# Order of GpSimd's work at the gate's maximum, and where the next pass's x operands are made, in an attention + MLP + mixture-of-experts kernel

## The chip, the cores and the metric

One Trainium2 chip, one of its cores. The time of a kernel is in microseconds of the device (us), the median of several executions. One further execution was taken with the hardware profiler, and every row below comes from that one.

## The reference

Three stages follow one another (2304 tokens, 512 features). The change lies in the third.

```python
x = block_causal_attention(q, k, v)          # 4 x 8 heads x 576 x 64 -> 2304 x 512
h = x @ w_in;  x = np.maximum(0.01 * h, h) @ w_out
# experts, E = 8, F = 1024
logits = x @ w_gate
logits = logits - logits.max()               # one maximum over all tokens and experts
P = np.exp(logits)
for _ in range(8):
    P /= P.sum(1, keepdims=True) + 1e-09
    P /= P.sum(0, keepdims=True) + 1e-09
    P *= N / E
for e in range(E):
    out += P[:, e:e+1] * (np.maximum(x @ w1[e], 0.0) @ w2[e])
```

## The kernel before, in words

All products are made from split operands: a value is kept as a high part (rounded by ScalarE) and a low part (the rest, by VectorE), and three matmuls stand for one. In the rows `xh…`, `w1h`, `w2h` are high parts and `xl…`, `w1l`, `w2l` low parts.

**Experts.** The tokens are cut into `NPASS` = 3 passes of 768. A group is an expert and a quarter of its F (256 columns); a pass has 32 groups, worked through in 16 rounds of two (`n` and `n + 1`, the loop at the end). A round has two halves. The *first products* (`first`, `product`, L851) make x @ w1 by a scheme with seven products in place of eight, so 14 products of 6 matmuls a round. Their x operands are called A11, S1, S2, S3, S4, A12 and A22 (`terms`); `x_step(p, k)` makes one of them for pass p: ScalarE's high part, VectorE's low part, and with `make` a VectorE subtraction of x blocks before it (`x_src`). `quarter` (first pass) takes the results "22", "12", "21" and "11" from PSUM: VectorE adds a kept part (L868, tile `c`), ScalarE makes the high part of the ReLU (L874), VectorE the low part (L875). The *second products* multiply by w2: in the first pass `combine` (L1075), six tiles of 12 matmuls a round into four PSUM banks; in the later passes `seventh` (L1019), seven products again, except in the last round of each pass (`closing`), which uses `combine`.

**Weights in the first pass.** w1 and w2 of each group are loaded raw, split, turned into the sums that the seven-product scheme wants, and also written to DRAM for the passes behind. For w2: `w2_load` fetches 512 KB into the one buffer that the group's parity has, `w2_split` makes high and low parts (L129, L130), `w2_more` makes four sums of quarters in place on GpSimd (L740 to L743), `w2_away` splits those sums (L782 ScalarE, L783 VectorE, two of each) and stores them with `keep_parts` (L703). Only then can `w2_load` of the group two further on reuse the buffer. All loads and stores are issued on SyncE's queue.

**The gate.** In the first round of pass one (`n == 0`) the last logits are made between the first products. `gate_max` (after product 3) reduces on VectorE (`gmax`, L653) and across partitions on GpSimd (`gall`, L654). `normal` then runs the exponential and the first row sums (L657 to L668), and the 8 normalisations follow between later matmuls.

**Order.** The program is written in one order, and a scheduler with a timing model of its own settles each engine's order, so an instruction can stand on its engine ahead of one that was written before it. TensorE's order is pinned by `in_order`. `tc.issue_after(t)` keeps what is written under it behind instruction t on t's engine; `behind(...)` does that with the last quarter's two instructions (`last_taken`), and `next_on` pins the order of the later passes. Each engine runs its queue in order.

Of the kernel before, what the change touches and what calls it, by code (L numbers as in the profile page):

```python
# [15 lines left out]
P = 128  # L16
# [20 lines left out]
def block_attention_mlp_moe(  # L37
# [15 lines left out]
    nc = tc.nc  # L53
# [50 lines left out]
    def w_load(which, e, j, pool=None):  # L104
        raw = (pool or rawpool).tile([P, 1024], F32, name="wraw", tag="wraw")
        f0 = 2 * j * P
        if which == 1:
            src = w1[e - 1][:, f0:f0 + 2 * P]
            nc.sync.dma_start(
                out=raw.rearrange("p (c f) -> p c f", c=KC), in_=src.rearrange("(c p) f -> p c f", p=P)  # L110
            )
        else:
            nc.sync.dma_start(
                out=raw.rearrange("p (j d) -> p j d", j=2),
                in_=w2[e - 1][f0:f0 + 2 * P, :].rearrange("(j p) d -> p j d", p=P),
            )
        w_raw[which, e, j] = raw
# [359 lines left out]
    turned = const.tile([P, 32], F32, name="ramp_t")  # L477
# [55 lines left out]
    for w in (1, 2):  # L533
# [22 lines left out]
    st = {  # L556
        n: const.tile([P, w], F32, name=n)
        for n, w in (("gmax", 1), ("gall", 1), ("gneg", 1), ("rs", TT), ("cs", E), ("cr", E))
    }
# [91 lines left out]

    def gate_max():
        nc.vector.tensor_reduce(out=st["gmax"], in_=pr, axis=AX.XY, op=ALU.max)  # L653
        nc.gpsimd.partition_all_reduce(st["gall"], st["gmax"], P, bass.bass_isa.ReduceOp.max)  # L654

    def gate_exp():
        nc.vector.tensor_scalar(out=st["gneg"], in0=st["gall"], scalar1=-1.0, scalar2=None, op0=ALU.mult)  # L657
# [35 lines left out]
    terms = ("A11", "S1", "S2", "S3", "S4", "A12", "A22")  # L693
# [20 lines left out]
    def w2_load(n):  # L714
        if n < N0:
            w_load(2, 1 + groups[n][1], groups[n][2], raw2[n % 2])
# [3 lines left out]
    def w2_split(n):  # L720
        if n < N0:
            key = (2, 1 + groups[n][1], groups[n][2])
            w2_raw[n] = w_raw[key]
            w_split(*key)
            parts = w_part[key]
            keep_parts(2, n, 0, [x[:, DM:DM + HD] for x in parts], HD, DM, DM + HD)
            keep_parts(2, n, 1, [x[:, 0:DM] for x in parts], DM, DM, 2 * DM)
            if groups[n][1:] in ((E - 1, NI - 2), (E - 1, NI - 1)):
                keep_parts(2, n, 2, parts, 2 * DM)
# [5 lines left out]
    def w2_more(n):  # L735
        if n >= N0:
            return
        raw = w2_raw[n]
        b21, b22, b11, b12 = (raw[:, c * HD:(c + 1) * HD] for c in range(4))
        nc.gpsimd.tensor_tensor(out=b11, in0=b12, in1=b11, op=ALU.subtract)  # L740
        nc.gpsimd.tensor_tensor(out=b12, in0=b22, in1=b12, op=ALU.subtract)
        nc.gpsimd.tensor_tensor(out=b22, in0=b22, in1=b11, op=ALU.subtract)
        nc.gpsimd.tensor_tensor(out=b21, in0=b22, in1=b21, op=ALU.subtract)  # L743

    def w2_away(n):
        if n >= N0:
            return
        raw = w2_raw.pop(n)
        for part, x in ((0, raw[:, DM:2 * DM]), (1, raw[:, 0:DM])):
            pool, tag = ((mpool, "th"), (rawpool, "wb"))[part]  # L750
            hi = pool.tile([P, DM], F32R, name=tag, tag=tag, bufs=1)
            lo = x.bitcast(F32R)
            halves(hi, lo, x)
            keep_parts(2, n, part, (hi, lo), DM, 0)
# [78 lines left out]
    def x_step(p, k, make=True):  # L833
        src = x_src(p, k, make)
        hi, lo = (xpart.tile([P, 2, HT], F32R, name=f"x{n}{k}", tag=f"x{n}{k}") for n in "hl")
        put = next_on if tails else lambda f, **k: f(**k)
        put(nc.scalar.copy, out=hi, in_=src)
        put(nc.vector.tensor_tensor, out=lo, in0=src, in1=f32(hi), op=ALU.subtract)
        bq[p, k] = (hi, lo)
# [43 lines left out]
    def behind(*steps):  # L883
        with ExitStack() as order:
            for t in last_taken:
                order.enter_context(tc.issue_after(t))
            for s in steps:
                s()
# [331 lines left out]
    turned = False  # L1220
    done = 0
    for n in range(0, NGR, 2):
        p, e, i = groups[n]
        turn = closing(n) and p + 1 < NPASS
        for m in range(done, len(first_products)):
            first(n, m)
            if n == 0 and 0 < m <= TC // 2:
                in_order(gate_chunk)(NPASS - 1, TC // 2 + m - 1, o_bank())
            if p == 0:
                if n == 0 and m == 2:  # L1230
                    w2_split(n + 1)
                if n == 0 and m == 4:
                    w2_more(n + 1)
                if m in ((1, 3) if n else (2, 8)):
                    w2_away(n + m // 3 % 2 if n else n + m // 8)
                    w2_load(n + 2 + (m // 3 % 2 if n else m // 8))
                if m == 5:
                    w1_sums(n + 2)
            if turned and 2 < m < 6:
                x_step(p, terms[m + 1])  # L1240
            if n == 0 and m == TC // 2:
                gate_max()
            if norm and m in ((2, 6) if n else (5,)):
                normal(o_bank)
            if not norm and not owed and rows_owed and m == 8:
                in_order(gate_rows)(o_bank, rows_owed.pop(0))
            if turn and p == 0 and m == 2:
                x_step(p + 1, "A11")
                for k in ("S1", "S3"):
                    x_src(p + 1, k, True)  # L1250
            if m == 5:
                for g in range(2):
                    w1_fetch(n + 2 + g, 0)
            if p and closing(n) and 7 <= m < 7 + TC:
                turn_back(order[m - 7])
        if done and m == 13:
            for g in range(2):
                w1_fetch(n + 2 + g, 0)
        for g in range(2):
            w1_fetch(n + 2 + g, 1)  # L1260
        if owed and not norm:
            behind(settle)
        if n == 4:
            nc.sync.dma_start(out=x_away, in_=xa[2])
        done = 0
        if p and not closing(n):
            for k in ("A11", "S2"):
                for g in range(2):
                    (parted if k == "A11" else summed)(n + g, k)
            for j in range(len(sevens)):  # L1270
                for c in range(2):
                    seventh(n, j, c)
                    beside_seventh(n, j, c)
                if j < 6:
                    first(n + 2, j)
                if closing(n + 2):
                    join(j)
                if j == 0 and groups[n + 2][1] != e:
                    row_load(p, e + 1)
                if j == 2:  # L1280
                    for g in range(2):
                        w2_fetch(n + 2 + g, 0)
            for g in range(2):
                w2_fetch(n + 2 + g, 1)
            if closing(n + 2) and p + 1 < NPASS:
                nc.sync.dma_start(out=xa[2], in_=x_away)
            done = 6
            turned = False
            continue
        more = [  # L1290
            lambda: (w1_s(n + 2), w1_a(n + 2)),
            lambda: (w1_sums(n + 3), w1_load(n + 4)),
            lambda: (w1_s(n + 3), w1_a(n + 3)),
            lambda: (w1_load(n + 5), w2_split(n + 2)),
            lambda: (w2_more(n + 2), w2_split(n + 3)),
            lambda: w2_more(n + 3),
        ]
        for m, t in enumerate(order):
            combine(n, t)
            if norm and m in (1, 4):  # L1300
                normal(h_bank)
            if p == 0:
                behind(more[m])
            if turn and p == 0 and m < 3:
                behind(lambda: x_step(p + 1, terms[m + 1], m == 1))
            if turn and p and m < 4:
                x_step(p + 1, terms[m], m == 2)
                if m == 0:
                    for k in ("S1", "S3"):
                        x_src(p + 1, k, True)  # L1310
        if turn:
            if p == 0:
                for pool in (raw2[1], mpool, raw2[0]):
                    pool.release()
                tpool = tc.alloc_tile_pool(name="tpool", bufs=1, reuse_waits="tile")
                lay_out()
            for part in range(2):
                for g in range(2):
                    w2_fetch(n + 2 + g, part)
            row_load(p + 1, 0)  # L1320
        turned = turn
# [33 lines left out]
```

## Time and profile before

| | |
|---|---|
| Time, median of 3 executions | 2084.09 us (2083.12 to 2084.18) |
| Time of the profiled execution | 2082.56 us |
| Its span, first to last instruction | 2080.7 us |
| TensorE busy | 2056.3 us, 99% of the span |
| VectorE, ScalarE, GpSimd busy | 1567.5, 836.7, 660.7 us |
| Mean granted TensorE clock | 0.996 of full speed |
| DMA | 436.88 MB, mean 210 GB/s |

The experts begin about 603 us into the span; the first pass ends at about 1127 us, the second at about 1602 us. Busy time says which engine worked; the waits say what it stood still for, and in order of time they say what stood ahead of what on an engine.

### The profile page before, as it was taken

The page shows a single profiled execution, that of the slowest core. Times are in us where ns is not written, and L with a number is a line of the kernel's source. Part 1 is how long each engine was busy: PE and PEld are TensorE (multiplying, and loading weights), DVE is VectorE, ACT ScalarE, POOL GpSimd, SP SyncE. Part 2 cuts the span into 40 slices and gives each one's busy share as a digit, 9 for nine tenths or more (in the row PEclk, how much of TensorE's full clock was granted, in tenths as well). Part 3 has the DMA queues.
Part 4 walks back from the last instruction along what each step waited for, and adds up shares of the span by engine and source line. Part 5 has one row for each costly group of instructions (what it writes and reads, how often), then busy time and mean ns, then how long its engine had stood idle before and what let it go on. Part 6 is the DMA issues. An engine that isn't in the chain of part 4 may idle for free.

```text
span 2080.7 us, 31734 instructions
## 1 busy us (share of the span) xinstructions
PE 2056.3 (99%) x11196; PEld 1883.0 (90%) x11196; DVE 1567.5 (75%) x2707; ACT 836.7 (40%) x1826; POOL 660.7 (32%) x642
## 2 busy tenths in 40 slices
PE   9999999999998999999999999999999999999999
PEld 6666898988887889889898999999999999999998
DVE  7877656565467887877876688888887788888886
ACT  7776332222344454454453432323333433233322
POOL 2322212131023545534541333323331333233321
PEclk9999999999998999999999999999999999999999
DMA  5553111010056888888988677777777677777772
GB/s 139 128 125 78 41 41 51 31 51 31 1 192 223 298 294 314 304 292 309 322 300 334 244 269 251 263 255 252 272 264 277 234 251 265 254 250 274 262 258 104
DMA packets 235742, 436.88 MB, mean 210 GB/s; under 512 B 77864, under 2 KB 114728, under 8 KB 235328
## 3 DMA queue, kind: packets, MB, share of 16 engines
q1 hardware_dynamic: 234384, 434.56, 60.3%
q8 instruction: 89, 1.46, 0.3%
q14 instruction: 69, 0.57, 0.1%
q10 hardware_dynamic: 1200, 0.30, 0.1%
HBM read 308.82 MB, written 125.95 MB: 209 GB/s over the span
## 4 chain that ended last, share of the span: by engine, by line
PE 92%; DVE 4%; issue 1%; DMA 1%; POOL 1%; ACT 1%; SPq 0%; DVEq 0%; POOLq 0%; ACTq 0%
PE h_ps L851 27%; PE o L1019 21%; PE o L1075 13%; PE o L519 9%; PE h_ps L499 9%; PE sc L317 4%; PE o L851 3%; PE tr L357 2%; PE av L382 2%; DVE xa L948 1%; PE qm L291 0%; DVE w1l L783 0%; DMA k_0h<-th 0%; PE km L297 0%; PE av L379 0%
## 5 line engine op out<-in xcount | busy, mean ns | idle before, releaser
L948 DVE TENSOR_TENSOR xa<-o,xa 128x384 f32<-128x384 f32 x392 | 215.9, 552 | 110.4 <-PE o L1019 106.3
L851 PE MATMUL h_ps<-xhS,w1h 128*128 128x384 f32 x768 | 257.9, 336 | 0.0
L851 PE MATMUL h_ps<-xhS,w1l 128*128 128x384 f32 x768 | 257.0, 335 | 0.0
L851 PE MATMUL h_ps<-xlS,w1h 128*128 128x384 f32 x768 | 256.9, 335 | 0.0
L948 POOL TENSOR_TENSOR xa<-xa 128x384 f32<-128x384 f32 x92 | 106.0, 1152 | 414.0 <-DVE xa L948 373.8
L948 ACT COPY places<-h_ps 128x384 f32<-128x384 f32 x192 | 92.3, 481 | 291.5 <-PE h_ps L851 223.8
L948 ACT CAST xllate<-xa 128x384 fp32r<-128x384 f32 x120 | 61.6, 514 | 280.4 <-POOL xa L948 280.4
L851 PE MATMUL h_ps<-xhA,w1h 128*128 128x384 f32 x448 | 152.4, 340 | 14.1 <-DVE c L868 12.9
L851 PE MATMUL h_ps<-xhA,w1l 128*128 128x384 f32 x448 | 150.9, 337 | 0.0
L851 PE MATMUL h_ps<-xlA,w1h 128*128 128x384 f32 x448 | 150.9, 337 | 0.0
L851 PEld LDWEIGHTS h_ps<-xlS,w1h 128*128 128x128 f32 x768 | 144.5, 188 | 0.0
L851 PEld LDWEIGHTS h_ps<-xhS,w1h 128*128 128x128 f32 x768 | 144.5, 188 | 0.0
L851 PEld LDWEIGHTS h_ps<-xhS,w1l 128*128 128x128 f32 x768 | 144.4, 188 | 0.0
L1075 PE MATMUL o<-w2h,xhlate 128*128 128x512 f32 x408 | 143.8, 391 | 0.0
L948 POOL TENSOR_TENSOR places<-places 128x384 f32<-128x384 f32 x60 | 61.0, 1017 | 251.3 <-DVE wa L948 234.6
L1075 PE MATMUL o<-w2h,xllate 128*128 128x512 f32 x384 | 133.9, 389 | 0.0
L765 POOL TENSOR_TENSOR wa<-wraw 128x256 f32<-128x256 f32 x32 | 30.6, 957 | 306.9 <-DVE w1l L783 277.5
L1019 PE MATMUL o<-xllate,w2h 128*128 128x384 f32 x480 | 124.1, 337 | 3.0 <-DVE xllate L948 2.9
L507 DVE TENSOR_TENSOR g<-h_ps,g 128x512 f32<-128x512 f32 (+1 forms) x80 | 50.9, 636 | 96.9 <-ACT g L506 96.6
L1019 PE MATMUL o<-xhlate,w2h 128*128 128x384 f32 x480 | 121.7, 334 | 0.0
L519 PE MATMUL o<-hh,w2h 128*128 128x512 f32 (+1 forms) x320 | 117.8, 368 | 0.0
L519 PE MATMUL o<-hh,w2l 128*128 128x512 f32 (+1 forms) x320 | 117.7, 368 | 0.0
(260 smaller groups left out, 5754.4 us busy)
## 6 DMA issues: line engine op xcount, KB each, us to landing
wraw<-in_moe_w_dram SPq DMA_DIRECT2D x64, 512.0 KB, 4.5
w1h<-k_1h SPq DMA_DIRECT2D x64, 512.0 KB, 5.3
w1l<-k_1l SPq DMA_DIRECT2D x64, 512.0 KB, 6.3
w2h<-k_1h SPq DMA_DIRECT2D x60, 512.0 KB, 6.0
w2l<-k_1l SPq DMA_DIRECT2D x60, 512.0 KB, 6.9
w1h<-k_0h SPq DMA_DIRECT2D x64, 384.0 KB, 4.0
w1l<-k_0l SPq DMA_DIRECT2D x64, 384.0 KB, 4.5
w2h<-k_0h SPq DMA_DIRECT2D x60, 384.0 KB, 4.5
```

Of the source, the lines that this page charges most:

```text
L317: nc.tensor.matmul(sc, qbd[p % 2][:, i, :], kT[p % 2][:, lo:hi], start=True, stop=True)
L357: nc.tensor.transpose(tr[:, s].rearrange("p h q -> p (h q)"), ex[p % 2][:, off[i] + c * P:off[i] + (c + 1) * P], ident,)
L382: nc.tensor.matmul(av[p][r, 512 + P * max(c - 1, 0):512 + S - P], lhsT, a[:, q0:, :], start=c == 0, stop=c == NKC - 1,)
L499: nc.tensor.matmul(ps[:, 0:n], w[:, c, cols], x, start=c == 0 and s == 0, stop=c == KC - 1 and s == 2,)
L507: nc.vector.tensor_tensor(out=g[:, 0:n], in0=ps[:, 0:n], in1=g[:, 0:n], op=ALU.max)
L519: nc.tensor.matmul(ps[:, 0:n], w[:, cut], h[:, 0:n], start=start and m == 0, stop=stop and m == 2)
L765: nc.gpsimd.tensor_tensor(out=one[:, 0], in0=a21, in1=a22, op=ALU.add)
L851: mm = nc.tensor.matmul(ps, w[:, c], x[:, c], start=first and c == 0 and s == 0, stop=c == 1 and s == 2, skip_group_check=True,)
L948: ins = f(*a, **k)
L1019: mm = nc.tensor.matmul(o, a, b, start=i == 0, stop=i == 5)
L1075: mm = nc.tensor.matmul(o, h, w, start=m == 0, stop=m == 11)
```

## The change

There are two parts. **At the gate's maximum:** `gate_max` returns GpSimd's instruction, and `w2_more(1)` is written behind it with `tc.issue_after`; `w2_away(1)` and `w2_load(3)` leave the first products of round 0 (place 8) and are written behind the last quarter of that round, ahead of its second products; `w2_split(3)` is written one place later. **The x operands:** in the last round of a pass, x_step for the next pass is called at each of the six tiles of the second products, in place of three (next pass one) or four (next pass two); what is left for the first products of the next pass is A22 of the last pass, at place 1; before, S4, A12 and A22 of both passes stood there, at places 3 to 5.

```diff
     def gate_max():
         nc.vector.tensor_reduce(out=st["gmax"], in_=pr, axis=AX.XY, op=ALU.max)
-        nc.gpsimd.partition_all_reduce(st["gall"], st["gmax"], P, bass.bass_isa.ReduceOp.max)
+        t = nc.gpsimd.partition_all_reduce(st["gall"], st["gmax"], P, bass.bass_isa.ReduceOp.max)
+        return getattr(t, "ins", t)
...
-                if n == 0 and m == 4:
-                    w2_more(n + 1)
-                if m in ((1, 3) if n else (2, 8)):
-                    w2_away(n + m // 3 % 2 if n else n + m // 8)
-                    w2_load(n + 2 + (m // 3 % 2 if n else m // 8))
+                if m in ((1, 3) if n else (2,)):
+                    w2_away(n + m // 3)
+                    w2_load(n + 2 + m // 3)
                 if m == 5:
                     w1_sums(n + 2)
-            if turned and 2 < m < 6:
-                x_step(p, terms[m + 1])
+            if turned and p > 1 and m == 1:
+                x_step(p, terms[6])
             if n == 0 and m == TC // 2:
-                gate_max()
+                with tc.issue_after(gate_max()):
+                    w2_more(1)
...
-            lambda: (w2_more(n + 2), w2_split(n + 3)),
-            lambda: w2_more(n + 3),
+            lambda: (w2_more(n + 2), None if n == 0 else w2_split(n + 3)),
+            lambda: (w2_split(n + 3) if n == 0 else None, w2_more(n + 3)),
         ]
+        if n == 0:
+            behind(lambda: (w2_away(1), w2_load(3)))
         for m, t in enumerate(order):
...
-            if turn and p == 0 and m < 3:
-                behind(lambda: x_step(p + 1, terms[m + 1], m == 1))
-            if turn and p and m < 4:
-                x_step(p + 1, terms[m], m == 2)
+            if turn and p == 0:
+                behind(lambda: x_step(p + 1, terms[m + 1], m not in (0, 2)))
+            if turn and p:
+                x_step(p + 1, terms[m], m not in (1, 3))
```

## Rows read from the trace of the kernel before

**Rows 1.** The page: busy us (share of the span) xinstructions of each engine.

```profile
PE 2056.3 (99%) x11196; PEld 1883.0 (90%) x11196; DVE 1567.5 (75%) x2707; ACT 836.7 (40%) x1826; POOL 660.7 (32%) x642
```

**Rows 2.** Waits of TensorE: waiting line, releaser, total us, times, longest us.

```profile
PE h_ps L851 <- DVE c L868: 12.9, 3, 7.9
PE o L1019 <- DVE xllate L948: 2.9, 4, 1.0
PE h_ps L851 <- DVE xa L948: 1.2, 2, 0.6
```

**Rows 3.** Timeline of TensorE: start us, us, instruction, [idle before <- releaser].

```profile
619.79 0.34 PE L851 MATMUL h_ps<-xhS,w1l 128*128 128x384 f32 x1
624.74 0.69 PE L851 MATMUL h_ps<-xhA,w1h 128*128 128x384 f32 x1 [4.61 <-DVE c L868]
...
634.92 0.69 PE L851 MATMUL h_ps<-xhA,w1h 128*128 128x384 f32 x1 [7.89 <-DVE c L868]
...
641.67 0.39 PE L1075 MATMUL o<-w2h,xhlate 128*128 128x512 f32 x1
```

**Rows 4.** Chain that ended last, one later round's two halves: start us, us, what.

```profile
848.52 14.58 PE h_ps L851 x84
863.10 16.36 PE o L1075 x72
```

**Rows 5.** Timeline of GpSimd from 600 us.

```profile
601.05 0.73 POOL L768 TENSOR_TENSOR wa<-wraw,wa 128x256 f32<-128x256 f32 x1
614.96 0.74 POOL L740 TENSOR_TENSOR wraw<-wraw 128x256 f32<-128x256 f32 x1 [13.18 <-PE o L622]
622.01 0.38 POOL L654 PARTITION_ALL_REDUCE gall<-gmax  x1 [6.32 <-issue]
629.26 0.71 POOL L741 TENSOR_TENSOR wraw<-wraw 128x256 f32<-128x256 f32 x1 [6.87 <-issue]
```

**Rows 6.** Timeline of VectorE around the gate's maximum.

```profile
615.06 0.30 DVE L653 TENSOR_REDUCE gmax<-pr 128x1 f32<-128x144 f32 x1
622.42 0.15 DVE L657 TENSOR_SCALAR gneg<-gall 128x1 f32<-128x1 f32 x1 [7.06 <-POOL gall L654]
...
624.14 0.55 DVE L868 TENSOR_TENSOR c<-h_ps,s 128x384 f32<-128x384 f32 x1
...
630.82 0.69 DVE L783 TENSOR_TENSOR wraw<-wraw,th 128x512 fp32r<-128x512 f32 x1 [5.82 <-POOL wraw L742]
...
643.79 0.56 DVE L875 SCALAR_TENSOR_TENSOR xllate<-c,xllate 128x384 fp32r<-128x384 f32 x1 [0.59 <-ACT xllate L874]
```

**Rows 7.** GpSimd's sequencer, lines L654 and L331: ns min/median/max, first and last start.

```profile
L654 POOLq MODIFY_POOL_CONFIG  x2: 11/11/11, 615.6 to 615.7; - x2
L331 POOLq MODIFY_POOL_CONFIG  x2: 11/11/11, 8.8 to 8.8; - x2
```

**Rows 8.** Timeline of GpSimd at the start of the kernel.

```profile
8.08 0.54 POOL L441 COPY vraw<-nought 64x128 f32<-64x128 f32 x2
12.42 0.20 POOL L331 TENSOR_TENSOR ssum<-ssum 128x1 f32<-128x1 f32 x1 [3.80 <-ACT ex L326]
```

**Rows 9.** Stretch of one us: us, busy (x) of PE, PEld, DVE, ACT, POOL, granted clock, DMA share, GB/s.

```profile
640.00:641.00 1.00, 1.00 (x7) 1.00 (x6) 0.17 (x1) 0.28 (x1) 0.00 (x0) 0.83 0.00 0
```

**Rows 10.** Timeline of VectorE and TensorE where pass two begins.

```profile
1137.11 0.96 DVE L948 TENSOR_TENSOR xlA<-xa,xhA 128x768 fp32r<-128x768 f32 x1 [0.90 <-ACT xhA L948]
1137.98 0.55 DVE L948 TENSOR_TENSOR xa<-h_ps,places 128x384 f32<-128x384 f32 x1
...
1138.68 0.41 PE L851 MATMUL h_ps<-xhA,w1h 128*128 128x384 f32 x1 [0.58 <-DVE xa L948]
```

**Rows 11.** VectorE in a pass's last second products: us, busy (x), granted clock, DMA share, GB/s.

```profile
1590.00:1602.00 12.00, 8.69 (x11) 1.00 0.39 147
```

**Rows 12.** Timeline of ScalarE in the second products of round 0.

```profile
645.83 1.99 ACT L129 CAST w2h<-wraw 128x1024 fp32r<-128x1024 f32 x2
```

**Rows 13.** DMA issues from 570 to 720 us: what, queue, count, KB each, median us to landing.

```profile
wraw<-in_moe_w_dram SPq DMA_DIRECT2D x15, 512.0 KB, 4.3
```

## The prediction

> **What bounds the kernel now.** Read the page first: TensorE is busy for 99% of the span [rows 1]. So only what TensorE stands still for, or runs slowly through, can be won, and the next view is its waits. There are three entries of weight [rows 2]: 12.9 us for VectorE's tile `c` in the first pass, and 2.9 and 1.2 us for VectorE's results on L948. In order of time, the first is nearly all in one place: 4.61 and 7.89 us in round 0 of the experts [rows 3]. The other two are at the beginnings of passes two and three; one of the six is shown [rows 10].
>
> How large is the hole in round 0? TensorE starts the last matmul of S4 for the first group at 619.79 and the second products at 641.67 [rows 3], 21.88 us. Between lie five products of 6 matmuls (A22 twice, S4, A12 twice), so 31 steps from start to start. An undisturbed round takes 14.58 us for 84 matmuls [rows 4], 0.1736 a step, so the steps need 5.38. **16.50 us are lost**: 12.50 of waiting and 4.00 of slow matmuls. The slow ones show as durations of 0.69 in place of 0.34 [rows 3], and a granted clock that comes back to full speed only in the stretch of 640 to 641 [rows 9].
>
> Who makes the hole? Follow VectorE [rows 6]. It has the maximum of each partition at 615.06 + 0.30 = 615.36, then stands for 7.06 us before `gneg`, because GpSimd's cross-partition maximum begins at 622.01 only. The `c` that releases TensorE first (624.14) is queued behind the row sums. GpSimd shows why it is late [rows 5]: it finished older work at 601.05 + 0.73 = 601.78, then stood 13.18 us before L740, the first of the four sums of `w2_more(1)`, which waits for w2's split. Only behind that come two configuration records [rows 7] and 6.32 us in which the profile names nothing, then the maximum. Afterwards another 6.87 us pass before L741. The second wait follows from that: `w2_away(1)` needs those sums, its subtraction stands on VectorE ahead of the quarters, and VectorE waits 5.82 us for GpSimd with the quarters behind it [rows 6].
>
> **The change, part 1: GpSimd's order.** With all four sums behind the maximum, GpSimd's queue after 601.78 holds the configuration, then the maximum. What matters is whether the configuration starts when the queue reaches it, or only with the maximum's data. The trace has one more case [rows 8]: at the kernel's start a copy ends at 8.08 + 0.54 = 8.62, the configuration records stand at 8.8 [rows 7], and the next operation runs at 12.42 after waiting for ScalarE. There the records did not wait for the operand; they ran 3.6 us ahead of the operation. So I take the configuration to begin at 601.8 and, at 6.32 us, to be over at 608.1, 7.3 us before `gmax`. That margin is the cover; if it is gone, up to 6.32 us come back (first rival). The bounds: nothing hidden, or all.
>
> The maximum then runs at about 615.4 and ends, at 0.38 us, at 615.8. From its end to the end of the first `c` took 624.69 − 622.39 = 2.30 us [rows 5, 6]; so `c` is there at 618.1. TensorE wants it at 619.97. Even 1.8 us more cost nothing. The later quarters then follow TensorE as in every other round; in the first pass those waited only 12.9 − 12.50 = 0.4 us in all.
>
> **Part 1: what is moved.** The way back of the configuration takes 6.87 us, from 615.8 to 622.7; four sums of about 0.74 us [rows 5] end near 626. `w2_away(1)` now stands behind the last quarter. In the old kernel that quarter ends 643.79 + 0.56 − 641.67 = 2.68 us into the second products; in the new one second products begin at 619.79 + 5.38 = 625.17, so it comes at 627.9, and the sums are ready for it. Its two subtractions (0.69 each [rows 6]) and two ScalarE copies no longer stand in a pause but beside the second products, which need VectorE and ScalarE only to empty PSUM and for the normalisation. That could cost 0 to 1.4 us; I take 0.6, since the normalisation is a chain that TensorE waits for and VectorE is well loaded there. Its two stores and `w2_load(3)` move with it on SyncE's queue: SyncE waits for the stores to land before it may issue the load (for a store of 256 KB I take at most the 4.3 us that a load of 512 KB needs [rows 13], then the load itself), with w1's stores and loads queued behind. Those loads serve the round after next, which has a whole round to absorb it. So part 1 gives 16.50 − 0.6 = 15.9 us.
>
> **Part 2: the x operands.** At the beginning of a pass VectorE makes S4, A12 and A22 in front of the first quarter: the last such operation starts at 1137.11 and the quarter's L948 sum at 1137.98 [rows 10], and TensorE waits. These are 4.1 us over both passes [rows 2]. Nothing is removed, only moved: three high parts, three low parts and one subtraction a pass, about 0.96 us each on VectorE [rows 10]. In the last second products VectorE has the room: before pass three 8.69 of 12 us are used [rows 11], and there only S4 and A12, 1.9 us, come in; A22 goes into a stretch where the first products have just begun and no quarter is due. No DMA moves: the row of gate values that is fetched for the next pass lands on blocks that S3 frees, and S3 stays where it was. The gain is between 0 (another wait takes over) and 4.1; I take 4.1, since the same quarters run without a wait in all other rounds of these passes: the entry for L1019 counts 4 waits and the one for L948 counts 2 [rows 2].
>
> **The sum.** 15.9 + 4.1 = 20.0 us off. Against the profiled execution's own time, 2082.56, that gives 2062.6. The median of the runs shown is 2084.09, 1.5 above it, so for a median I say 2064.1, in round numbers **2064**.
>
> **The rivals.** *The configuration is paid at the call.* If it starts only once `gmax` is there, the maximum comes at 615.4 + 6.32 = 621.7, 0.3 us earlier than now. The first wait stays: TensorE resumes at 624.4 in place of 624.74, at the lower of its two clock levels (1.2 GHz). In the old kernel 24 matmuls after the last resumption took 641.67 − 634.92 = 6.75 us with the slow clock in them; the five products would take 6.75 + 6 × 0.1736 = 7.8, ending at 632.2. Part 1 then gives 9.5 us, less 0.6, and the time is 2084.1 − 8.9 − 4.1 = 2071. For it: at 615.6 records and idle time fit both readings, since `gmax` was ready by then. Against it: the start of the kernel, though there the configuration may have had nothing to do. 18%.
>
> The Trainium skill speaks for this rival: "GPSIMD Engine Reference", section "Instruction dispatch", says that the first call to a freshly loaded kernel pays an instruction load of about 6 us in addition. By that rule the time would be this rival's; the trace's 6.32 us agree with the size and leave open when it starts.
>
> *A stall once in the second products of round 0.* In the old order the high parts of w2 for groups 2 and 3 stand on ScalarE at 645.83 [rows 12], 4.2 us into the second products, ahead of copies that empty PSUM. If the scheduler leaves them there, ScalarE waits for `w2_load(3)`, which now lands at about 2.7 + 2 + 4.3 + 4.3 = 13.3 us (2 for the two splits, an estimate from the 0.69 of one subtraction and its copy; 4.3 at most for the stores). TensorE has four banks and wants the first one back after four of six tiles, 16.36 × 4 / 6 = 10.9 us [rows 4]. With 1 us for the high part that is waited for, that is 3.4 us of waiting, and slow matmuls of up to as much again: 2067.5 to 2071. The change writes `w2_split(3)` later, which speaks against it. 10%.
>
> *Part 2 gives nothing*, another wait standing behind the one removed: 2068.1. 10%.
>
> *Slower: the odd groups' buffer becomes the pace of the first pass.* Load, split, sums, splits, stores share one buffer. If the late `w2_load(3)` put this circle behind TensorE for good, each of the 15 rounds left would pay; from 20.0 / 15 = 1.33 us a round on the kernel is slower, and 2 us a round give 2064 + 30 = 2094. Against it: from round 2 on the order written is the old one, and a delay that is hung on the last quarter of one round is paid once. 5%.
>
> **How the numbers follow.** The forecast has 57%, with its own range of 2062 to 2066 (all of it won, or 1.4 us more lost beside the second products, and a spread between executions of 1). The others end at 2068, 2069, 2071 and 2094. To leave out no more than 2 in 10, the range must reach the first rival: 2061.5 to 2071.5. A measurement of this kernel tells 0.2%, 4.2 us, from no change; all cases but the last lie beyond that on the fast side. Faster 0.93, same 0.02, slower 0.05.
>
> **What would show it.** Right: configuration records near 602 and not 615.6; `gneg` before 616.5; no wait of TensorE above 1 us and a clock of 1.00 from 615 to 645; second products at about 625; no wait on L1019 at the beginnings of the passes. Wrong: idle time named "issue" between `gmax` and the maximum; ScalarE standing before w2's high part with the copies to empty PSUM behind it; waits of TensorE that recur in every round of the first pass.

## The result, and the profile after

The changed kernel takes 2062.72 us (median of 4 executions, 2060.87 to 2063.26); the kernel before, beside it, 2084.14 (4 executions, 2083.12 to 2084.30). The ratio is 0.9897, 95% interval 0.9880 to 0.9914: 21.4 us less. The forecast was 2064, 1.3 us above. The profiled execution took 2062.46 us; the old one's 2082.56 less the forecast's 20.0 is 2062.56. Its span fell by 20.1 us to 2060.6. The lines of the new kernel are those of the old one plus one, from L655 on.

The page first, engine by engine as in [rows 1], and the line of the 40 slices that matters (the clock in tenths of full speed). TensorE is busy for the whole span, and its clock shows full speed in every slice.

```profile
PE 2052.5 (100%) x11196; PEld 1880.4 (91%) x11196; DVE 1565.5 (76%) x2707; ACT 836.3 (41%) x1826; POOL 660.2 (32%) x642
...
PEclk9999999999999999999999999999999999999999
```

TensorE's waits, the answer to [rows 2]. The 12.9 us for `c` are 0.3, and both entries of L948 (now L949) are gone. One line has grown: four waits, 1.4 us in all, for the column sums of the normalisation (L674); the old kernel lists one of 0.3 there (L673).

```profile
PE o L674 <- DVE cs L669: 1.4, 4, 0.6
PE warm L253 <- POOL still L427: 1.0, 1, 1.0
PE h_ps L852 <- DVE c L869: 0.3, 1, 0.3
```

The hole of [rows 3]: the timeline of TensorE from the last matmul of S4 to the first of the second products.

```profile
620.54 0.33 PE L852 MATMUL h_ps<-xhS,w1l 128*128 128x384 f32 x1
620.71 0.33 PE L852 MATMUL h_ps<-xhA,w1h 128*128 128x384 f32 x1
...
625.91 0.39 PE L1076 MATMUL o<-w2h,xhlate 128*128 128x512 f32 x1
```

From 620.54 to 625.91 are 5.37 us for 31 steps, 0.1732 each, against 21.88 us before: all 16.5 us of the hole are closed. (Everything in this profile stands 0.75 us later before the gate; 619.79 has become 620.54.) The window from 615 to 645 says the same of the clock: its mean was 0.72 and is 1.00. Columns as in [rows 9], first before, then after.

```profile
615.00:645.00 30.00, 17.50 (x75) 16.08 (x74) 10.97 (x26) 7.60 (x17) 3.74 (x5) 0.72 0.32 114
615.00:645.00 30.00, 30.00 (x155) 27.11 (x155) 24.54 (x50) 15.62 (x31) 12.68 (x16) 1.00 0.72 249
```

GpSimd, beside [rows 5] and [rows 7]: its configuration records, and its timeline around the maximum.

```profile
L654 POOLq MODIFY_POOL_CONFIG  x2: 11/11/11, 602.5 to 602.5; - x2
L741 POOLq MODIFY_POOL_CONFIG  x2: 82/82/83, 616.6 to 616.6; - x2
```

```profile
601.78 0.74 POOL L769 TENSOR_TENSOR wa<-wraw,wa 128x256 f32<-128x256 f32 x1
616.25 0.38 POOL L654 PARTITION_ALL_REDUCE gall<-gmax  x1 [13.72 <-DVE gmax L653]
625.21 0.73 POOL L741 TENSOR_TENSOR wraw<-wraw 128x256 f32<-128x256 f32 x1 [8.58 <-ACT xllate L875]
...
628.05 0.74 POOL L744 TENSOR_TENSOR wraw<-wraw 128x256 f32<-128x256 f32 x1
```

The records stand at 602.5, where the work before ends (601.78 + 0.74), and no longer at 615.6. The 13.72 us of standing are now a wait for `gmax`, not "issue". Two more records, those of L741, stand right behind the maximum, as they did before (622.3): there the way back begins. VectorE, beside [rows 6], has `gmax` at 616.10 and `gneg` 0.56 us later; before, it stood 7.06 us there. (`gneg` at 616.66 misses the forecast's sign, before 616.5, by 0.16; the whole profile stands 0.75 later.)

```profile
615.80 0.30 DVE L653 TENSOR_REDUCE gmax<-pr 128x1 f32<-128x144 f32 x1
616.66 0.16 DVE L658 TENSOR_SCALAR gneg<-gall 128x1 f32<-128x1 f32 x1 [0.55 <-POOL gall L654]
```

**Where the rest went.** Three stretches hold the change between the two profiles; a round is called by its `n`, so round 2 follows round 0. A runs from the first matmul of the experts' first products to the second products of round 0, B from there to the second products of round 6, C from there to the last second products of all (starts read from TensorE's timeline and chain).

| kernel | A | B | C | time, median |
|---|---|---|---|---|
| before | 38.16 | 96.54 | 1321.9 | 2084.1 |
| after | 21.65 | 98.55 | 1315.9 | 2062.7 |

A gives 16.51, B takes 2.01 back, and C gives 6.0, 20.5 in all. The span fell by 20.1, since the new profile stands 0.75 later before A and ends 0.36 sooner behind C; the medians differ by 21.4. B is the grown line for L674 and what stands around it; the experiments return to it. C holds both pass beginnings and is larger than the 4.1 us of [rows 2]: compared matmul by matmul, the two beginnings alone are 2.86 and 2.87 us shorter, 5.7 together.

### The profile page after: what moved, and what is told of

Read it like the earlier page. It is cut to its first block, busy times and chain, and to the rows that moved or that the text cites. A ratio compares the mean times of both kernels' runs of the same rounds, so it can differ in the third digit from the quotient of the medians.

```text
span 2060.6 us, 31742 instructions
## 1 busy us (share of the span) xinstructions
PE 2052.5 (100%) x11196; PEld 1880.4 (91%) x11196; DVE 1565.5 (76%) x2707; ACT 836.3 (41%) x1826; POOL 660.2 (32%) x642
## 4 chain that ended last, share of the span: by engine, by line
PE 93%; DVE 3%; DMA 1%; POOL 1%; issue 1%; ACT 1%; SPq 0%; DVEq 0%; POOLq 0%; ACTq 0%
PE h_ps L852 28%; PE o L1020 21%; PE o L1076 12%; PE o L519 9%; PE h_ps L499 9%; PE sc L317 4%; PE o L852 3%; PE av L382 2%; PE tr L357 2%; DVE xa L949 1%; DMA k_1h<-wb 0%; PE qm L291 0%; PE km L297 0%; PE av L379 0%; PE l_ps L633 0%
## 5 line engine op out<-in xcount | busy, mean ns | idle before, releaser
L949 DVE TENSOR_TENSOR xa<-o,xa 128x384 f32<-128x384 f32 x392 | 215.9, 552 | 111.2 <-PE o L1020 107.0
L852 PE MATMUL h_ps<-xhS,w1h 128*128 128x384 f32 x768 | 257.5, 335 | 0.0
L852 PE MATMUL h_ps<-xhS,w1l 128*128 128x384 f32 x768 | 256.6, 334 | 0.0
L852 PE MATMUL h_ps<-xlS,w1h 128*128 128x384 f32 x768 | 256.6, 334 | 0.0
L949 POOL TENSOR_TENSOR xa<-xa 128x384 f32<-128x384 f32 x92 | 106.1, 1153 | 408.6 <-DVE xa L949 371.3
L949 ACT COPY places<-h_ps 128x384 f32<-128x384 f32 x192 | 92.3, 481 | 287.4 <-PE h_ps L852 219.8
L949 ACT CAST xllate<-xa 128x384 fp32r<-128x384 f32 x120 | 61.7, 514 | 280.0 <-POOL xa L949 280.0
L852 PE MATMUL h_ps<-xhA,w1h 128*128 128x384 f32 x448 | 150.9, 337 | 0.3 <-DVE c L869 0.3
L852 PE MATMUL h_ps<-xhA,w1l 128*128 128x384 f32 x448 | 149.9, 335 | 0.0
L852 PE MATMUL h_ps<-xlA,w1h 128*128 128x384 f32 x448 | 149.9, 335 | 0.0
L852 PEld LDWEIGHTS h_ps<-xhS,w1h 128*128 128x128 f32 x768 | 144.2, 188 | 0.1
L852 PEld LDWEIGHTS h_ps<-xlS,w1h 128*128 128x128 f32 x768 | 144.2, 188 | 0.0
L852 PEld LDWEIGHTS h_ps<-xhS,w1l 128*128 128x128 f32 x768 | 144.2, 188 | 0.0
L949 POOL TENSOR_TENSOR places<-places 128x384 f32<-128x384 f32 x60 | 60.9, 1015 | 251.1 <-DVE wa L949 234.4
L1020 PE MATMUL o<-xllate,w2h 128*128 128x384 f32 x480 | 123.1, 337 | 0.1
L1020 PE MATMUL o<-xhlate,w2h 128*128 128x384 f32 x480 | 121.8, 334 | 0.0
```

The lines of the kernel that those rows point to most:

```text
L852: mm = nc.tensor.matmul(ps, w[:, c], x[:, c], start=first and c == 0 and s == 0, stop=c == 1 and s == 2, skip_group_check=True,)
L949: ins = f(*a, **k)
L1020: mm = nc.tensor.matmul(o, a, b, start=i == 0, stop=i == 5)
```

## The experiments

All times are medians, beside the kernel before on the same chip (2083.16 for e1 to e4; 2082.70 for e5, e6, e8 and e9; 2082.86 for e7, e10 and e11). The stretches come from one profiled execution each. For e6 that one took 2068.56 us (its three others 2064.18 to 2064.51) and for e1 2070.24, so their stretches hold more loss than their medians.

| run | A | B | C | time |
|---|---|---|---|---|
| e1 gate part alone | 21.66 | 99.16 | 1323.5 | 2068.52 |
| e2 x part alone | 38.35 | 96.32 | 1315.5 | 2076.35 |
| e3 sums behind the maximum only | 32.29 | 96.15 | 1315.2 | 2070.01 |
| e4 w2_away later only | 28.90 | 97.36 | 1316.4 | 2069.95 |
| e5 configuration at the call | 29.24 | 97.77 | 1315.4 | 2068.10 |
| e6 w2_away(1) without its split | 21.65 | 104.76 | 1316.4 | 2064.36 |
| e7 w2_split(3) at its old place | 21.68 | 98.22 | 1315.7 | 2061.04 |
| e8, e11 maximum by TensorE | 22.68, 22.68 | 97.21, 97.16 | 1315.3, 1315.8 | 2060.95, 2060.99 |
| e9 w2_away(1) later still | 21.68 | 99.83 | 1316.4 | 2063.19 |
| e10 w2_away behind the column sums | 21.68 | 99.78 | 1315.3 | 2062.14 |

**e1 and e2: each part alone.** e1 is the changed kernel with the old calls of `x_step`, e2 the old kernel with the new ones:

```diff
-            if turned and 2 < m < 6:
-                x_step(p, terms[m + 1])
+            if turned and p > 1 and m == 1:
+                x_step(p, terms[6])
...
-            if turn and p == 0 and m < 3:
-                behind(lambda: x_step(p + 1, terms[m + 1], m == 1))
-            if turn and p and m < 4:
-                x_step(p + 1, terms[m], m == 2)
+            if turn and p == 0:
+                behind(lambda: x_step(p + 1, terms[m + 1], m not in (0, 2)))
+            if turn and p:
+                x_step(p + 1, terms[m], m not in (1, 3))
```

> Part 1 alone: the gate's order and w2's moves as changed, the x operands as before. The whole change took 21.4 us off (2084.1 to 2062.7). If the waits at the beginnings of passes two and three cost what the view of the waits lists (4.1 us), this kernel takes 2066.8; if they cost what TensorE's starts show between the two traces (2.87 and 2.86 us, 5.7 together), it takes 2068.4.

> Part 2 alone: the x operands as changed, the gate as before. By the listed waits 2084.1 - 4.1 = 2080.0; by TensorE's starts 2084.1 - 5.7 = 2078.4. The hole of 16.5 us in round 0 should be there unchanged in either case. If the parts hang together in another way, this and part 1 alone do not add up to 21.4.

The gate part alone gives 14.6 us (2068.52; ratio 0.9930, 0.9916 to 0.9943), the x part alone 6.8 (2076.35; 0.9967, 0.9954 to 0.9979). Together they make 21.4, the whole of the change, so within the spread of the medians the parts do not disturb each other. e1 came out where the starts of matmuls had put it (2068.4), not the listed waits (2066.8). e2 lies 2.0 below the nearer of its two values (2078.4); 0.9 of that is the kernel before, which took 2083.16 here and not 2084.1. In e1 the six waits are as before, and one of them shows why they cost more than they are listed at (timeline of TensorE at the beginning of pass two, e1):

```profile
1123.71 0.34 PE L852 MATMUL h_ps<-xhS,w1l 128*128 128x384 f32 x1
1124.63 0.41 PE L852 MATMUL h_ps<-xhA,w1h 128*128 128x384 f32 x1 [0.58 <-DVE xa L949]
1124.88 0.34 PE L852 MATMUL h_ps<-xlA,w1h 128*128 128x384 f32 x1
1125.05 0.34 PE L852 MATMUL h_ps<-xhA,w1l 128*128 128x384 f32 x1
```

From start to start these are 0.92 and 0.25 us, where undisturbed ones are 0.17. So 0.83 us are lost, while the listing counts 0.58, from the modelled end of the matmul before. With this 0.25 more for each of six waits, an estimate from the one, 4.1 becomes 5.6, beside the 5.7 by which the two beginnings became shorter. C of e2 is 6.4 below C of before; such a difference is uncertain by 1 or 2 (C of e1 and of before, with the same order there, differ by 1.6).

**e3 and e4: the gate part cut in two.** e3 keeps the sums of group 1 behind the maximum, with `w2_away(1)`, `w2_load(3)` and `w2_split(3)` at their old places. e4 has those three at the new places and the sums at the old one.

```diff
 e3
-                if m in ((1, 3) if n else (2,)):
-                    w2_away(n + m // 3)
+                if m in ((1, 3) if n else (2, 8)):
+                    w2_away(n + m // 3 % 2 if n else n + m // 8)
...
-        if n == 0:
-            behind(lambda: (w2_away(1), w2_load(3)))
 e4
+                if n == 0 and m == 4:
+                    w2_more(n + 1)
...
-                with tc.issue_after(gate_max()):
-                    w2_more(1)
+                gate_max()
```

> Only the four sums stand behind the maximum; w2_away(1), w2_load(3) and w2_split(3) are at their old places; x operands as changed. My theory: the first wait goes, since the configuration runs ahead, but the second stays, since w2_away(1) still stands on VectorE ahead of the quarters and its sums now come only after the way back of the configuration (at 623 to 625 us). TensorE then resumes near 629 to 631 at the lower clock and needs 6.75 us: about 10 to 12 us over the changed kernel, 2073 to 2075. Rival: the sums alone cure both waits, 2063.

> Only w2_away(1), w2_load(3) and w2_split(3) move; w2_more(1) is written at its old place and may stand ahead of the maximum; x operands as changed. My theory: the configuration starts only after w2's split again, so the first wait of 4.6 us stays and the clock falls; the second wait is gone. TensorE resumes at about 624.7, 30 matmuls take 7.8 us: 6.6 to 7.5 us over the changed kernel, 2069.3 to 2070.5. Rival: moving w2_away(1) is what counts and the order before the maximum does not, 2063.

e3 takes 2070.01 (0.9936, 0.9922 to 0.9949), e4 2069.95 (0.9936, 0.9923 to 0.9950). e4 came out as expected; e3 lies between its two theories. In A it is the first theory, in size too: of the 16.5 us, 5.9 go and 10.6 stay (32.29 against 21.65; 10 to 12 were expected). The time is only 7.3 above the changed kernel because B, with `w2_away(1)` at its old place, is 2.4 shorter (96.15 against 98.55) and C 0.7. VectorE's timeline in e3 shows what stays. The first `c` is there in time, but `w2_away(1)`'s subtraction stands ahead of the quarter's next operations and waits for sums that come only after the way back from the configuration:

```profile
618.17 0.56 DVE L869 TENSOR_TENSOR c<-h_ps,s 128x384 f32<-128x384 f32 x1
618.64 0.42 DVE L669 TENSOR_REDUCE cs<-pr 128x8 f32<-128x144 f32 x1
625.52 0.69 DVE L784 TENSOR_TENSOR wraw<-wraw,th 128x512 fp32r<-128x512 f32 x1 [6.46 <-POOL wraw L743]
626.13 1.08 DVE L876 SCALAR_TENSOR_TENSOR xhlate<-c,xhlate 128x384 fp32r<-128x384 f32 x1
```

TensorE waits 7.91 us for the next `c`, which stands behind it. The waits of TensorE in e3, and in e4, where the other wait stays alone:

```profile
PE h_ps L852 <- DVE c L869: 7.9, 1, 7.9
```

```profile
PE h_ps L852 <- DVE c L869: 4.9, 2, 4.3
```

So the two waits of [rows 3] have two causes, and each edit removes one: the place of the sums the first, the place of `w2_away(1)` the second (9.3 us of A). Neither alone is worth the whole.

**e5: the configuration made to start at the call.** A copy on GpSimd, which needs `gmax`, stands ahead of the maximum, and the maximum reads the copy.

```diff
-        t = nc.gpsimd.partition_all_reduce(st["gall"], st["gmax"], P, bass.bass_isa.ReduceOp.max)
+        nc.gpsimd.tensor_copy(out=st["cr"][:, 0:1], in_=st["gmax"])
+        t = nc.gpsimd.partition_all_reduce(st["gall"], st["cr"][:, 0:1], P, bass.bass_isa.ReduceOp.max)
```

> The changed kernel with one GpSimd copy of gmax (128 x 1) put between gmax and the maximum, which then reads the copy. The copy costs about 0.2 us, but it holds the configuration back until gmax is there. If the configuration otherwise runs ahead, it now stands on the path: records at 616 and not at 602, the maximum some 6.3 us later, the first wait of 4.6 us and the lower clock back, about 7 us over the changed kernel: 2069.7. If it is paid at the call in any case, or not on the path, the time stays at 2062.7 to 2063.2.

It takes 2068.10 (0.9929, 0.9914 to 0.9944), 5.4 to 7.1 us more than the order of the changed kernel (2062.72, and 2061.04 in e7); A alone is 7.6 longer, B and C a little shorter. The records follow the copy, and the maximum comes 6.2 us behind them (e5: the sequencer's records, GpSimd's timeline, TensorE's window):

```profile
L655 POOLq MODIFY_POOL_CONFIG  x2: 11/11/11, 615.7 to 615.7; - x2
```

```profile
615.56 0.19 POOL L654 COPY cr<-gmax 128x1 f32<-128x1 f32 x1 [13.66 <-DVE gmax L653]
621.92 0.38 POOL L655 PARTITION_ALL_REDUCE gall<-cr  x1 [6.18 <-DMA wraw<-in_moe_w_dram]
```

```profile
624.00:632.00 8.00, 7.35 (x25) 7.05 (x26) 5.11 (x11) 2.87 (x6) 2.77 (x4) 0.57 0.01 2
```

(The profile puts the end of the 6.18 us down to a DMA; in e4, in e2 and before, where it names none, the same gap is 6.04, 6.59 and 6.32.) TensorE waits 4.39 us once, and from 624 to 632 its granted clock is 0.57: this is the first rival, built. Its forecast was 7.0 us lost in the hole (16.5 less 9.5); 7.6 were.

**e6 and e9: does the moved work itself cost?** In e6 `w2_away(1)` stores its sums as they are, in both parts, with neither ScalarE's copy nor VectorE's subtraction; in e9 it and `w2_load(3)` stand behind the third tile of the second products.

```diff
 e6
+            if n == 1:
+                keep_parts(2, n, part, (lo, lo), DM, 0)
+                continue
             halves(hi, lo, x)
```

> The changed kernel without the two ScalarE copies and two VectorE subtractions of w2_away(1); the raw sums are stored in place of both parts, so the stores and w2_load(3) keep their bytes and places (the values that passes two and three use for that one group are then not split). Some 2.0 us of the hole are given back in rounds 2 and 4, where TensorE waits for the column sums. If that comes from this work on VectorE in the second products of round 0, these waits go and the time falls by 1 to 2 us, to 2061; if from SyncE's queue and the later load, it stays at 2062.7.

> The changed kernel with w2_away(1) and w2_load(3) written behind the third tile of the second products in place of ahead of the first. If what is given back comes from w2_away(1) delaying the low part of w2 for group 2, and with it GpSimd's sums that VectorE then waits for ahead of the normalisation, this order gives some of the 2 us back: 2061 to 2062. If any place in the second products costs VectorE the same, 2062.7; if the load of group 3 comes late, over 2064.

Neither is faster, so both expectations of a gain fell: e6 takes 2064.36 (0.9917, 0.9902 to 0.9932), e9 2063.19 (0.9905, 0.9889 to 0.9922). e9 is later with w2, and B grows to 99.83; TensorE's one listed wait for the column sums is 2.0 us there. e6 has four operations less, and yet B grows to 104.76. With the work gone the scheduler chose other orders. On SyncE's queue two of the four stores of `w2_away(1)` now stand ahead of `w2_load(2)`, which is issued at 625.86 in place of 617.72. On GpSimd a sum of w1, which stands 9.24 us for VectorE, is ahead of the first of w2's group 2 (e6, timeline), and VectorE waits 3.38 us for that group ahead of the column sums:

```profile
642.17 0.74 POOL L769 TENSOR_TENSOR wa<-wraw 128x256 f32<-128x256 f32 x1 [9.24 <-DVE pr L682]
642.86 0.74 POOL L741 TENSOR_TENSOR wraw<-wraw 128x256 f32<-128x256 f32 x1
643.56 0.81 POOL L770 TENSOR_TENSOR wa<-wa,wraw 128x256 f32<-128x256 f32 x1
...
645.71 0.72 POOL L772 TENSOR_TENSOR wa<-wraw,wa 128x256 f32<-128x256 f32 x1
646.39 0.72 POOL L743 TENSOR_TENSOR wraw<-wraw 128x256 f32<-128x256 f32 x1
```

TensorE then waits, and starts again slowly (e6, timeline and the window behind it):

```profile
648.31 0.36 PE L674 MATMUL o<-cs,ones 128*128 128x8 f32 x2 [2.79 <-DVE cs L669]
649.51 0.69 PE L855 MATMUL h_ps<-xhS,w1h 128*128 128x384 f32 x1 [0.84 <-ACT s L863]
```

```profile
649.50:656.00 6.50, 6.49 (x22) 6.49 (x23) 4.01 (x12) 2.58 (x7) 3.46 (x4) 0.55 0.71 270
```

e6 therefore does not price the four operations: it changed the order with them, and how much each of the two new orders costs was not separated. What it shows is that leaving the operations out doesn't bring B back, and that TensorE's wait there is one for w2's sums of the next groups.

**e10: the subtraction held behind the column sums.** In the changed kernel VectorE stands in round 2 as in e6, only shorter. The same subtraction in the kernel before, where it does not stand, is the first line; then VectorE in the changed kernel, and the matmul that waits for it:

```profile
658.95 0.68 DVE L783 TENSOR_TENSOR wraw<-wraw,th 128x512 fp32r<-128x512 f32 x1
```

```profile
642.39 1.21 DVE L784 TENSOR_TENSOR wraw<-wraw,th 128x512 fp32r<-128x512 f32 x1 [1.64 <-POOL wraw L743]
643.52 0.84 DVE L682 TENSOR_TENSOR pr<-pr,cr 128x144 f32<-128x144 f32 x1
...
645.86 0.42 DVE L669 TENSOR_REDUCE cs<-pr 128x8 f32<-128x144 f32 x1
```

```profile
646.42 0.36 PE L674 MATMUL o<-cs,ones 128*128 128x8 f32 x2 [0.35 <-DVE cs L669]
```

```diff
-                    w2_away(n + m // 3)
+                    if n in (2, 4):
+                        with tc.issue_after(sums_made[-1]):
+                            w2_away(n + m // 3)
+                    else:
+                        w2_away(n + m // 3)
```

(`sums_made` holds the column sums' instructions, L669.)

> The changed kernel, with VectorE's subtractions of w2_away in rounds 2 and 4 kept behind the column sums that the next normalisation step needs; nothing else is pinned. In the changed kernel the second products of round 0 begin 98.6 us before those of round 6, 2.0 us more than the 96.5 of the old kernel, and TensorE waits four times for the column sums there (0.35, 0.16, 0.59, 0.26). If it is this place on VectorE's queue that gives the 2.0 us back, the two waits at the beginnings of rounds 2 and 4 go (0.35 and 0.59), the stretch falls to 96.5 to 97.3 us and the time to 2060.7 to 2061.9. If the later load is what costs (the ring of buffers, whatever stands where), something else waits in its place and the time stays at 2062.7.

The two waits are gone, and nothing is won: 2062.14 (0.9900, 0.9885 to 0.9915), B 99.78. In their place TensorE waits for ScalarE, twice directly (1.1 us) and once for a `c` (1.2) that stands on VectorE behind a wait of 1.97 for ScalarE (e10: TensorE's waits from 612 to 745 us, then ScalarE and VectorE):

```profile
PE h_ps L854 <- DVE c L871: 1.2, 1, 1.2
PE h_ps L854 <- ACT s L862: 1.1, 2, 0.9
PE o L676 <- DVE cs L670: 0.6, 2, 0.4
```

```profile
679.23 0.62 ACT L785 CAST wb<-wraw 128x512 fp32r<-128x512 f32 x1 [1.67 <-POOL wraw L746]
679.76 0.47 ACT L862 COPY s<-h_ps 128x384 f32<-128x384 f32 x1
...
718.36 0.69 DVE L786 TENSOR_TENSOR wraw<-wraw,wb 128x512 fp32r<-128x512 f32 x1 [1.97 <-ACT wb L785]
```

ScalarE's high part of the same sums waits for GpSimd too, with the copy that empties PSUM behind it. My theory, that the place on VectorE's queue gives the time back, fell; the rival's form holds, late sums that stall whichever queue they reach first.

**e7: `w2_split(3)` at its old place.**

```diff
-            lambda: (w2_more(n + 2), None if n == 0 else w2_split(n + 3)),
-            lambda: (w2_split(n + 3) if n == 0 else None, w2_more(n + 3)),
+            lambda: (w2_more(n + 2), w2_split(n + 3)),
+            lambda: w2_more(n + 3),
```

> The changed kernel with w2_split(3) written at its old place, one tile earlier. The rival of a stall in the second products of round 0 (ScalarE standing at w2's high part with the copies that empty PSUM behind it) says 2 to 8 us slower, 2065 to 2071. If the scheduler puts ScalarE's work in the same order in either case, the time is that of the changed kernel, 2062.7, and this edit of the diff did nothing.

2061.04 (0.9895, 0.9880 to 0.9909), with the waits of the changed kernel. The scheduler made the same order of instructions on every engine as without this edit, so the edit did nothing, and e7 is a second sample of the changed kernel's order: 2061.0 and 2062.7. The kernel before took 2082.86 beside the one and 2084.14 beside the other, so the ratios are 0.9895 and 0.9897.

**e8 and e11: no cross-partition operation on GpSimd.** TensorE turns `gmax` (a matmul with the identity), VectorE takes the maximum of the row, a matmul with ones spreads it; w2's work stays where it was in the old kernel, and the exponential comes two products later.

```diff
-        t = nc.gpsimd.partition_all_reduce(st["gall"], st["gmax"], P, bass.bass_isa.ReduceOp.max)
+        mm = nc.tensor.transpose(ps[0:1, 0:P], st["gmax"], ident)
+        nc.vector.tensor_reduce(out=st["cr"][0:1, 0:1], in_=ps[0:1, 0:P], axis=AX.X, op=ALU.max)
...
+        mm = nc.tensor.matmul(ps[:, 0:1], ones[0:1, :], st["cr"][0:1, 0:1], start=True, stop=True)
+        nc.vector.tensor_copy(out=st["gall"], in_=ps[:, 0:1])
```

> The maximum across partitions by TensorE (a transposition of gmax, VectorE's maximum of the row, a matmul with a row of ones that spreads it), so GpSimd is not configured at all and w2_more(1), w2_away(1), w2_load(3), w2_split(3) stand at their old places; the exponential is two places later; x operands as changed. Theory: no wait in round 0, two more small matmuls (0.3 us each), and the 2 us that are given back in rounds 2 and 4 are kept: 2061 to 2062. Rival: w2's work at its old place crowds the quarters, or the chain over TensorE comes late: 2063 or more.

> The kernel whose maximum is found by TensorE and VectorE, once more, beside the changed kernel's order on the same chip. If it is really faster than the changed kernel (by its first run, 2060.95 against 2062.7 on another chip), it stays 1 to 2.5 us below the run with w2_split(3) at its old place, if that one runs as the changed kernel does. By the stretches of their profiles alone it should be near 0.3 us below: 1.0 us more in round 0, 1.3 us less up to round 6.

2060.95 and 2060.99 (0.9896 and 0.9894): e11, beside e7's 2061.04 on the same chip, shows no difference. It pays 1.0 us in A (two small matmuls and the gaps around them) and wins it back in B.

## Why the prediction was right, point by point

**The hole** held to the hundredth: 16.50 were forecast, 16.51 came. It had been worked out from starts of matmuls, with the slow ones in it, not from listed waits (12.50).

**The start of the configuration**, the forecast's one real choice, fell as taken: when the queue reaches it. The records at 602.5 and the maximum 0.15 us behind `gmax` show it; e5, where an instruction that needs `gmax` stands ahead, brings back 615.7 and 6.18 us. The first rival (18%) is thereby excluded for this order, and priced nearly right where it holds: 2071 was said, 2068.1 measured. Of the difference 2.4 are C's (6.5 gained in e5, not 4.1) and 1.4 the kernel before, which took 2082.70 beside e5; A and B took 1.2 back. The Trainium skill, "GPSIMD Engine Reference", section "Instruction dispatch", says that the first call to a freshly loaded kernel pays about 6 us. These traces agree with the size (6.18 in e5; 6.04 and 6.59 in e4 and e2, where a sum of w2 stands ahead of the maximum). They do not bear out the rival's reading of it, that this is paid once the operation's data are there: with the queue free it was over by then, beside other work (0.15 us from `gmax` to the maximum).

**The way back** was put at 6.87 us; here it took 8.58 (616.25 + 0.38 to 625.21). The six other profiles with the sums right behind the maximum (e1, e3, e6, e7, e9, e10) show 7.0 to 7.3. The profile puts the end of the 8.58 down to ScalarE's `xllate`, which ends 0.06 us before, so part of it may be a wait for ScalarE; no run settles that. The last sum ends at 628.79, and ScalarE asks for its result at 629.01, so even 8.58 were hidden, by 0.2 us.

**What is moved** was put at 0.6 us, bounds 0 to 1.4. This is the mis-sized term: B lost 2.0 us here, 1.7 in e7 and 2.6 in e1. The place was mistaken too: not beside the second products of round 0, where the two copies and two subtractions run without a wait of TensorE, but in rounds 2 and 4, at the column sums. I had written that w2's load has a whole round to absorb its delay; it has not quite. Two things seem to add up. e8 and e11, without the hole but with w2's work at its old places, lose 0.6 to 0.7 in B; that TensorE, with the hole gone, no longer gives GpSimd and the loads time to get ahead is an inference that no run tests alone. The later `w2_away(1)` and load go with the rest, 1.0 to 2.0 (B of after, e7 and e1 against e8's). That lateness of w2's sums is the cause is shown by VectorE's wait of 1.64 us for them ahead of the column sums, which the kernel before does not have, and by e10 (the wait moves with the queue). e9 fits (later still, and B grows by 1.3), though its time is only 0.5 above that of the changed kernel. How much falls to the stores, the load and SyncE's queue each was not separated.

**The x operands** were put at 4.1 us by listed waits; 5.7 came at the two beginnings, 6.0 to 6.4 in C, 6.8 by e2's time. The mechanism was right, and the waits on L1020 and L852 at the pass beginnings are gone. The size was read from the wrong measure: two parts of one forecast used two, starts for the hole and listed idle time here.

**The other rivals.** No stall in the second products of round 0: ScalarE makes w2's high parts at 631.71 and 642.72, each with its data there. The reason given against it was no reason, as e7 shows: the edit did not change the order. Nothing recurs round by round, B is paid once, and the odd groups' buffer is no pace. Part 2 gave something.

That the time came so near is partly luck: the two errors, 1.4 too little loss in B and about 1.9 too little gain in C, nearly cancelled. Part by part, 15.9 and 4.1 us were forecast, and 14.6 (e1) and 6.8 (e2) came. The rest of the 1.3 us between 2064 and 2062.72 lies within what two samples of one order differ by (1.7).

## What to carry to other kernels

Read a stall on TensorE from start to start of its matmuls: here a listed wait missed about 0.25 us for a short pause, and all of the slow matmuls behind a long one (12.5 listed, 16.5 lost). The 6 us of configuration ahead of GpSimd's maximum were free here because nothing that must wait stood between the end of its earlier work and it, and 13.7 us lay between. So look at what is ahead of such an operation in the queue, not only at when its data come, and at what waits for the way back behind it. And when a hole in the critical engine closes, look at the rounds after: here late preparation of w2 gave 2 of the 16.5 us back.

## What was not expected of the hardware

The way back from the cross-partition maximum took 8.58 us in one profile and 7.01 in another of the same order. In both the DMA engines were full at its beginning (share 1.06 and 1.01, to 619); from 619 to 623 the share was 0.57 in the first and 0.33 in the second. Whether that makes the difference, or the wait for ScalarE that the profile names, was not tried.

After waits of 2.79 and 0.84 us in the profiled execution of e6 (2068.56 us, where the median is 2064.36) the granted clock was 0.55 over 6.5 us, near the lower of TensorE's two levels (1.2 of 2.4 GHz); in the changed kernel, with single waits of 0.35 and less in the same round, it stayed at 1.00. From the second products of round 0 to those of round 2 this execution took 38.61 us, 5.7 more than the changed kernel (32.92), with 3.6 us of listed waiting.
